# A d-transform with its even half folded a second time, and its copies moved from VectorE to ScalarE

## The chip, the cores and the metric

The kernel runs on one core of one Trainium2 chip. The metric is the device time of one execution in microseconds (us); the median of the runs is given. The profile's engines are PE (TensorE matmuls), PEld (TensorE weight loads), DVE (VectorE), ACT (ScalarE), POOL (GpSimd) and SP (SyncE, which here issues most transfers).

## What is computed

The input x has 2048 rows (time steps) of 1024 columns (d). Two results are made from it and mixed row by row with a gate:

```python
def reference(A_x, A_w_r, A_w_i, B_x, B_Lambda_re, ..., gate_w):
    x = A_x
    g = _sigmoid((x * gate_w).sum(-1, keepdims=True))
    a = irfft2(rfft2(x) * (A_w_r + 1j * A_w_i))        # over rows and columns
    # b: Bu = x @ B_bar^T; h[t] = Lam_bar * h[t-1] + Bu[t]; b = 2 Re(h @ C^T) + x * Dskip
    b = _B_ref(x, B_Lambda_re, ...)
    return g * a + (1 - g) * b
```

Branch a is a spectral filter (a two-dimensional Fourier transform, a product, and the way back). Branch b is a linear recurrence over 2048 steps with 1024 complex states.

## The kernel before

All transforms are matmuls with constant matrices in bf16; sums are in fp32 in PSUM.

**The front of branch a**, about the first 87 us, takes x in 16 row groups of 128 rows, j = 0 to 15. For each group:

- `turn_x(j)`: eight PE transposes (L666) put columns on partitions, into a PSUM tile `pt` (two buffers), and one ACT copy (L667) brings it into `xQ`.
- `fold(j)`: two DVE operations form lo + hi (L674) and lo - hi (L675) of the two halves of d, 128x512 elements each, into a tile `preT` (three buffers). The sum is what the even frequencies need, the difference what the odd ones need.
- `fd(j)`, the d-transform: eight PE matmuls (L346) of 512 columns. For each class (0 even, 1 odd) four blocks of 128 folded columns are multiplied with the constant `G_sb` and summed in one half of the PSUM tile `ps_fd`. A copy (L349) brings it in natural order of frequencies into `X1`; it is on DVE for j = 3, 5, 7 and on ACT for the others.
- `s1(j)`: four PE matmuls (L358), the first step of the transform over rows. A copy (L363) brings it from PSUM into `A1`: on DVE for j below 8, on ACT from 8 on. SP stores A1 to DRAM (L365). The A1 of groups 0 to 7 lie in `CT[0]`, space that x used before; those of 8 to 15 take four places in turn, so that group 12 overwrites group 8. Before that, `keep_A1` (DVE, L369 and L371) saves one column of each into `Acol`.

The PSUM pool `psA` has two buffers, which fd and s1 take in turn: fd(j+1) waits for the copy of fd(j), and s1(j+1) for the copy of s1(j).

**Around it.** The order is written out by hand: `plan` says for each step j of `front()` in which order transposes (T), folds (f), fd(j+1) (F) and s1(j) (S) are issued, and every engine works through its instructions in that order. Among these steps stand the tables of branch b (`make_tab`, four times: DVE L215, L828, L830, L232, L237; ACT L832, L833, L835, L226, L231; casts on POOL, L222 and L228). After step 8, halves of branch b's units are issued in between as well.

**Branch b** is cut into eight chunks of 256 steps. `unit(c, q)` is two times 32 matmuls of 256 columns (L308, `psu`), each followed by an ACT copy (L310). `recur` then queues the DVE work of that chunk (products with the tables, L263 and L266; scans, L278; the way back, L288 and L291). `vector(us)` takes pieces from this queue, by costs written beside them, and so fixes at build time where they stand between the folds. `early(tb)` and the later output tiles read the finished states with PE (`ps_y`, L580); the first such read needs all of chunk 0.

**SP's queue** carries, in order: x and G and T2 (the constant of s1), then the stores of A1 between the transposing loads of B (L207) and C (L565), then the loads of W and of the next constants.

Of the kernel before, what the change touches and what calls it, by code (L numbers as in the profile page):

```python
# [14 lines left out]
BF16 = mybir.dt.bfloat16  # L15
# [22 lines left out]
def _host_consts():  # L38

    d = np.arange(K)[:, None] + 0.5  # L40
    G = np.zeros((2, K, 2, H))
    for cls in range(2):
        k = 2 * np.arange(H)[None, :] + cls
        ang = 2 * np.pi * d * k / D
        G[cls, :, 0] = np.cos(ang)
        G[cls, :, 1] = -np.sin(ang)
    G[0, :, 1, 0] = (-1.0) ** np.arange(K)

    n = np.arange(H)[None, :] + 0.5
    Gi = np.zeros((2, 2, 2, P, H))  # L50
    for cls in range(2):
        for kb in range(2):
            k = 2 * (P * kb + np.arange(P)[:, None]) + cls
            ang = 2 * np.pi * k * n / D
            Gi[cls, kb, 0] = 2.0 * np.cos(ang)
            Gi[cls, kb, 1] = -2.0 * np.sin(ang)
    Gi[0, 0, 0, 0] = 1.0
    Gi[0, 0, 1, 0] = (-1.0) ** np.arange(H)
    Gi /= float(D * S)
    pf = np.arange(P)  # L60
    s1 = (32 * (pf % 64) + 16 * (pf // 64))[:, None, None]
# [36 lines left out]
    return dict(  # L98
        G=b16(G.reshape(2, 4, P, K).transpose(2, 0, 1, 3)),
        Gi=b16(Gi.reshape(8, P, H).transpose(1, 0, 2)),  # L100
        T2=b16(np.concatenate([Ts, Tc, -Ts], axis=2)),
        K3=b16(np.stack([Kc, Ks], axis=1)),
        MT=b16(np.concatenate([-Mim, Mre, Mim], axis=2)),
        KRS=b16(np.concatenate([K2, R2, Sel.reshape(P, 4 * P)], axis=1)),
        JP=b16(np.stack([J, P0], axis=1)),
    )
# [3 lines left out]
def kernel(  # L110
# [17 lines left out]
    nc = tc.nc  # L128
# [4 lines left out]
    cG = nc.inline_tensor(hc["G"], name="c_G").ap()  # L133
# [29 lines left out]
    pre = ictx.enter_context(tc.tile_pool(name="pre", bufs=1, side="right"))  # L163
    gta = ictx.enter_context(tc.tile_pool(name="gta", bufs=2, side="right"))
# [27 lines left out]
    fft["G"] = pre.tile([P, 2, 4, K], BF16, name="G_sb")  # L192
    raw = t3p.tile([P, 6 * D], BF16, name="raw")
    fft["T2"] = raw[:, 0:3 * D].rearrange("p (j m) -> p j m", m=192)

# [141 lines left out]
    def gfnet():  # L337
        T2_sb, G_sb = fft["T2"], fft["G"]
# [2 lines left out]

        def fd(j):
            ps = psA.tile([P, 2, K], FP32, name="ps_fd", tag="ps")
            for cls in range(2):
                for d4 in range(4):
                    nc.tensor.matmul(ps[:, cls, :], lhsT=preTs[j][:, 4 * cls + d4, :], rhs=G_sb[:, cls, d4, :],  # L346
                                     start=(d4 == 0), stop=(d4 == 3))
            X1 = gta.tile([P, 2, K], BF16, name="X1")
            (nc.vector.tensor_copy if j in (3,5,7,) else nc.scalar.copy)(out=X1.rearrange("p r (i c) -> p r i c", c=2), in_=ps.rearrange("p c (r i) -> p r i c", r=2))  # L349
            X1s[j] = X1  # L350

        def s1(j):
            X1 = X1s.pop(j)
            psa = psA.tile([P, 2, K], FP32, name="ps_s1", tag="ps")
            for r in range(2):
                for g in range(2):
                    half = slice(64 * g, 64 * (g + 1))
                    nc.tensor.matmul(psa[:, g, :], lhsT=T2_sb[half, j, 64 - 64 * r:192 - 64 * r], rhs=X1[half, r, :],  # L358
                                     start=(r == 0), stop=(r == 1), tile_position=(64 * g, 0))
# [3 lines left out]
            (nc.vector.tensor_copy if j < 8 else nc.scalar.copy)(out=A1, in_=psa)  # L363
# [294 lines left out]
        yield 3.9  # L658


    preTs = {}

    def turn_x(j):
        pt = psX.tile([P, 8, P], BF16, name="pt")
# [3 lines left out]
                       in_=pt.rearrange("p d (c q g) -> p d c g q", c=NCH, g=2))  # L668

    def fold(j):  # L670
        preTs[j] = gta.tile([P, 8, P], BF16, name="preT", bufs=3)
        lo, hi = (x_gjq[:, :, d:d + 4, :, j, :].rearrange("p c d g q -> p d g c q") for d in (0, 4))
        to = preTs[j].rearrange("p d (g c q) -> p d g c q", g=2, c=NCH)
        nc.vector.tensor_add(out=to[:, 0:4], in0=lo, in1=hi)  # L674
        nc.vector.tensor_sub(out=to[:, 4:8], in0=lo, in1=hi)  # L675
# [308 lines left out]
```

## Time and profile before

| | us |
|---|---|
| median of 3 runs (339.67 to 341.55) | 340.32 |
| the profiled execution | 340.26 |
| its span, first to last instruction | 338.5 |

| engine | busy us | share of the span | instructions |
|---|---|---|---|
| PE | 327.9 | 97% | 2446 |
| PEld | 212.0 | 63% | 2446 |
| DVE | 283.5 | 84% | 385 |
| ACT | 167.3 | 49% | 211 |
| POOL | 32.7 | 10% | 64 |

Busy is the time in which an engine runs an instruction; waiting is not busy. On DVE and ACT an instruction starts shortly before the one ahead of it ends, so what a further one costs is the step from start to start, and not its duration. A line of a timeline gives start, duration, engine, line, operation, output and input, and in brackets how long the engine stood idle before it and who released it. The groups that the change touches:

| line, engine, operation | count | mean or median ns of one |
|---|---|---|
| L346 PE matmul ps_fd, 512 columns | 128 | 379 |
| L308 PE matmul psu, 256 columns | 1024 | 273 |
| L674, L675 DVE preT, 128x512 | 16 + 16 | 417, 418 |
| L349 copy of ps_fd on ACT, 128x1024 | 13 | 1012 |
| L349 copy of ps_fd on DVE | 3 | 1215 |
| L363 copy of ps_s1 on DVE, 128x1024 | 8 | 1218 |
| L363 copy of ps_s1 on ACT | 8 | 1018 |

### The profile page before, as it was taken

How to read it: one execution, taken by the hardware profiler on the slowest of the kernel's cores; microseconds unless marked ns; L12 is line 12 of the kernel's file. 1: busy time of each engine (PE TensorE's matmuls, PEld its weight loads, DVE VectorE, ACT ScalarE, POOL GpSimd, SP SyncE). 2: the span in 40 equal slices, each digit the busy share in tenths (PEclk: the TensorE clock that was granted, in tenths of full speed). 3: DMA queues.
4: the chain of work that ended last, by engine and by line, in shares of the span. 5: the costliest groups of instructions: out<-in, count | busy, mean ns of one | idle time of the engine just before them, and what ended most of it. 6: DMA issues, size and time to landing. Idle time of an engine off the chain costs nothing.

```text
span 338.5 us, 6167 instructions
## 1 busy us (share of the span) xinstructions
PE 327.9 (97%) x2446; PEld 212.0 (63%) x2446; DVE 283.5 (84%) x385; ACT 167.3 (49%) x211; POOL 32.7 (10%) x64
## 2 busy tenths in 40 slices
PE   8989899979999999999999999999999999999995
PEld 3445465656985574847566575869945876565552
DVE  2679948999999999999997999199699939999741
ACT  3697598836241245656557452546632243433510
POOL 1382011140000000000000000000000011121410
PEclk9999999999999999999999999999999999999999
DMA  7999999999890346899999955898114004556892
GB/s 268 404 200 144 244 220 213 129 202 263 261 230 11 95 123 145 254 243 282 259 270 242 218 174 151 225 188 217 62 33 122 35 4 71 102 86 124 131 194 102
DMA packets 83581, 58.71 MB, mean 173 GB/s; under 512 B 54328, under 2 KB 74304, under 8 KB 83424
## 3 DMA queue, kind: packets, MB, share of 16 engines
q1 hardware_dynamic: 80304, 55.64, 66.5%
q0 software_dynamic: 3168, 2.66, 8.3%
q8 instruction: 19, 0.31, 0.4%
q14 instruction: 10, 0.08, 0.1%
q10 hardware_dynamic: 80, 0.01, 0.0%
HBM read 30.49 MB, written 17.83 MB: 143 GB/s over the span
## 4 chain that ended last, share of the span: by engine, by line
PE 81%; DVE 13%; ACT 3%; issue 2%; ACTq 0%; DVEq 0%
PE ps_y L580 29%; PE psu L308 28%; PE ps_h L580 4%; PE ps_id L611 4%; PE ps_fd L346 3%; PE ps_is L519 2%; PE ps_is L494 2%; PE ps_s L470 2%; PE ps_is L495 2%; DVE CT L363 2%; PE ps_y L584 2%; DVE h L278 1%; DVE preT L674 1%; PE psw L684 1%; DVE preT L675 1%
## 5 line engine op out<-in xcount | busy, mean ns | idle before, releaser
L308 PE MATMUL psu<-xQ,BT 128*128 128x256 bf16 x1024 | 116.2, 273 | 0.8 <-ACT ye L598 0.5
L308 PEld LDWEIGHTS <-BT 128*128 128x128 bf16 x1024 | 99.0, 98 | 17.4 <-issue 4.5
L580 PE MATMUL ps_y<-CT,h 128*128 128x512 bf16 x448 | 101.3, 379 | 0.0
L580 PEld LDWEIGHTS <-h 128*128 128x128 bf16 x512 | 49.4, 98 | 55.3
L278 DVE TENSOR_TENSOR_SCAN h<-rz,h 128x1024 bf16<-128x1024 f32 x32 | 71.9, 2278 | 0.2
L310 ACT CAST h<-psu 128x1024 bf16<-128x1024 f32 x32 | 32.3, 1010 | 51.0 <-PE psu L308 51.0
L263 DVE TENSOR_TENSOR xQ<-h,tab 128x4096 bf16<-128x4096 bf16 x12 | 27.4, 2287 | 14.2 <-ACT h L310 14.2
L266 DVE TENSOR_TENSOR h<-h,tab 128x4096 bf16<-128x4096 bf16 (+1 forms) x20 | 37.3, 1864 | 0.8
L626 POOL DMA_DIRECT2D BT<-y_scratch x10 | 11.9, 1194 | 238.8 <-DVE BT L620 227.1
L598 ACT ACTIVATE ye<-ps_y,omg 128x512 f32<-128x512 f32 x20 | 12.7, 684 | 43.4 <-PE ps_y L584 35.7
L346 PE MATMUL ps_fd<-G_sb,preT 128*128 128x512 bf16 x128 | 30.4, 379 | 1.6 <-ACT X L349 1.0
L346 PEld LDWEIGHTS <-preT 128*128 128x128 bf16 x128 | 12.0, 97 | 15.5 <-issue 2.8
L472 ACT CAST X<-ps_s 128x1024 bf16<-128x1024 f32 x16 | 16.2, 1014 | 8.7 <-PE ps_s L470 8.7
L667 ACT COPY xQ<-pt 128x1024 bf16<-128x1024 bf16 x16 | 15.6, 1016 | 2.6 <-PE pt L666 2.5
L521 ACT CAST ZT<-ps_is 128x1024 bf16<-128x1024 f32 x16 | 15.5, 1024 | 2.2 <-PE ps_is L519 2.2
L497 ACT CAST C<-ps_is 128x1024 bf16<-128x1024 f32 x16 | 16.1, 1007 | 0.0
L611 PE MATMUL ps_id<-raw,ZT 128*128 128x256 bf16 x128 | 15.9, 273 | 0.0
L349 ACT CAST X<-ps_fd 128x1024 bf16<-128x1024 f32 x13 | 13.2, 1013 | 5.5 <-PE ps_fd L346 5.4
L580 PE MATMUL ps_h<-CT,h 128*128 128x512 bf16 x64 | 14.5, 379 | 0.0
L611 PEld LDWEIGHTS <-ZT 128*128 128x128 bf16 x128 | 12.4, 98 | 2.2
L674 DVE TENSOR_TENSOR preT<-xQ 128x512 bf16<-128x512 bf16 x16 | 7.4, 460 | 5.8 <-ACT xQ L667 5.8
L494 PE MATMUL ps_is<-X,raw 128*128 128x512 bf16 x32 | 12.1, 379 | 0.0
(189 smaller groups left out, 350.0 us busy)
## 6 DMA issues: line engine op xcount, KB each, us to landing
y_scratch<-ye SPq DMA_DIRECT2D x20, 256.0 KB, 2.7
CT<-in_A_x_dram SPq DMA_DIRECT2D x8, 512.0 KB, 5.6
Bb<-turn_scratch SPq DMA_DIRECT2D x16, 256.0 KB, 3.8
turn_scratch<-C SPq DMA_DIRECT2D x16, 256.0 KB, 4.5
raw<-turn_scratch SPq DMA_DIRECT2D x16, 256.0 KB, 4.7
Wb<-in_A_w_r_dram SPq DMA_DIRECT2D x32, 127.8 KB, 4.0
Wb<-in_A_w_i_dram SPq DMA_DIRECT2D x32, 127.8 KB, 3.8
out_dram<-BT SPq DMA_DIRECT2D x14, 256.0 KB, 2.6
```

What stands on the lines that cost most here:

```text
L263: nc.vector.tensor_mul(out=tmps["s"], in0=u[:, ::-1], in1=bc(i))
L266: nc.vector.tensor_mul(out=u, in0=u, in1=bc(i))
L278: nc.vector.tensor_tensor_scan(out=seg, data0=rz[:, js.start + j:js.start + j + 4].rearrange("p j t -> p (j t)"), data1=seg, initial=0.0, ...
L308: nc.tensor.matmul(psu[:, j, :], lhsT=BT[4 * q + j][:, ri, d8, :], rhs=xQ[:, c, d8, :], start=(d8 == 0), stop=(d8 == 7))
L310: nc.scalar.copy(out=hs[c][:, ri, 4 * q:4 * q + 4].rearrange("p b (q j) -> p b q j", j=32), in_=psu.rearrange("p b (j q) -> p b q j", j=32))
L346: nc.tensor.matmul(ps[:, cls, :], lhsT=preTs[j][:, 4 * cls + d4, :], rhs=G_sb[:, cls, d4, :], start=(d4 == 0), stop=(d4 == 3))
L472: nc.scalar.copy(out=X2, in_=ps2)
L494: nc.tensor.matmul(psc[:, h, :], lhsT=MT_sb[:, b, 64:192], rhs=UV[0][:, h, :], start=True, stop=False)
L497: nc.scalar.copy(out=C1.rearrange("p h (c i) -> p h c i", c=2), in_=psc.rearrange("p h (i c) -> p h c i", c=2))
L580: nc.tensor.matmul(psy, lhsT=hs[c][:, ri, jb, P * tq:P * (tq + 1)], rhs=CT[ri][:, jb, 512 * dh:512 * (dh + 1)], start=(i == 0), stop=False)
L611: nc.tensor.matmul(pse[:, slot, :], lhsT=ZT_t[:, i, tb, :], rhs=fft["Gi"][:, i, :], start=(kb == 0), stop=(kb == 1))
L667: nc.scalar.copy(out=x_gjq[:, :, :, :, j, :].rearrange("p c d g q -> p d c g q"), in_=pt.rearrange("p d (c q g) -> p d c g q", c=NCH, g=2))
```

## The change

The even frequencies are split once more. From the sum s = lo + hi (four blocks of 128 columns) a second fold makes s_lo + s_hi, for the frequencies 4m, and s_lo - s_hi, for 4m + 2. Each of the two needs only two blocks and gives 256 outputs. The even half of fd thus becomes four matmuls of 256 columns in place of four of 512; the odd half stays, and now comes first. The constant `G_sb` is laid out anew, and its second transfer is half as large (256 KB). The copy into `X1` reads PSUM in a new order (two by two, from both classes and both even parts).

The second fold is done for two groups at once: for groups 0 and 1 two operations of 128x256 each, and from then on two operations of 128x2x256 after every odd group. fd of an even group therefore waits for the fold of the next group. `preT` becomes a tile for two groups (two buffers), and the sums have a tile of their own (one buffer).

All X1 copies are on ACT (before, 3, 5 and 7 were on DVE), and the A1 copies of groups 1, 3, 5, 7 too (before, all below 8 were on DVE). `plan` is as it was.

```diff
-                nc.tensor.matmul(ps[:, cls, :], lhsT=preTs[j][:, 4 * cls + d4, :], rhs=G_sb[:, cls, d4, :],
-                                 start=(d4 == 0), stop=(d4 == 3))
+            for d4 in range(4):
+                nc.tensor.matmul(ps[:, 1, :], lhsT=preTs[j][:, 4 + d4, :], rhs=Go[:, d4, :], start=(d4 == 0), stop=(d4 == 3))
+            for e in range(2):
+                for d2 in range(2):
+                    nc.tensor.matmul(ps[:, 0, H * e:H * (e + 1)], lhsT=preTs[j][:, 2 * e + d2, :], rhs=Ge[:, e, d2, :],
+                                     start=(d2 == 0), stop=(d2 == 1))
...
-            (nc.vector.tensor_copy if j in (3,5,7,) else nc.scalar.copy)(out=X1.rearrange("p r (i c) -> p r i c", c=2), in_=ps.rearrange("p c (r i) -> p r i c", r=2))
+            (nc.vector.tensor_copy if j in () else nc.scalar.copy)(
+                out=X1.rearrange("p r (m e c) -> p r m e c", e=2, c=2),
+                in_=ps.rearrange("p c (e r m) -> p r m e c", e=2, r=2))
...
-            (nc.vector.tensor_copy if j < 8 else nc.scalar.copy)(out=A1, in_=psa)
+            (nc.vector.tensor_copy if j in (0, 2, 4, 6) else nc.scalar.copy)(out=A1, in_=psa)
...
     def fold(j):
-        preTs[j] = gta.tile([P, 8, P], BF16, name="preT", bufs=3)
+        if j % 2 == 0:
+            pairs["t"] = gta.tile([P, 2, 8, P], BF16, name="preT", bufs=2)
+            pairs["s"] = gta.tile([P, 2, 4, P], BF16, name="sums", bufs=1)
+        preTs[j] = pairs["t"][:, j % 2]
         lo, hi = (x_gjq[:, :, d:d + 4, :, j, :].rearrange("p c d g q -> p d g c q") for d in (0, 4))
-        to = preTs[j].rearrange("p d (g c q) -> p d g c q", g=2, c=NCH)
-        nc.vector.tensor_add(out=to[:, 0:4], in0=lo, in1=hi)
-        nc.vector.tensor_sub(out=to[:, 4:8], in0=lo, in1=hi)
+        apart = lambda t: t.rearrange("p d (g c q) -> p d g c q", g=2, c=NCH)
+        nc.vector.tensor_sub(out=apart(preTs[j])[:, 4:8], in0=lo, in1=hi)
+        nc.vector.tensor_add(out=apart(pairs["s"][:, j % 2]), in0=lo, in1=hi)
+        rs = slice(j % 2, j % 2 + 1) if j < 2 else slice(0, 2)
+        if j < 2 or j % 2:
+            s_lo, s_hi = pairs["s"][:, rs, 0:2], pairs["s"][:, rs, 2:4]
+            nc.vector.tensor_add(out=pairs["t"][:, rs, 0:2], in0=s_lo, in1=s_hi)
+            nc.vector.tensor_sub(out=pairs["t"][:, rs, 2:4], in0=s_lo, in1=s_hi)
...
-    for cls in range(2):
-        nc.sync.dma_start(out=fft["G"][:, cls], in_=cG[:, cls])
+    for part in (slice(0, 4 * K), slice(4 * K, 4 * K + 4 * H)):
+        nc.sync.dma_start(out=fft["G"][:, part], in_=cG[:, part])
```

More of the change, by code (lines that the diff above doesn't have):

```diff
@@ L47, in _host_consts @@
     G[0, :, 1, 0] = (-1.0) ** np.arange(K)
+    Ge = np.stack([G[0, :H, :, e::2] for e in range(2)])
+    Go = np.stack([G[1, :, :, e::2] for e in range(2)], axis=1)
     n = np.arange(H)[None, :] + 0.5
@@ L98, in _host_consts @@
     return dict(
-        G=b16(G.reshape(2, 4, P, K).transpose(2, 0, 1, 3)),
+        G=b16(np.concatenate([Go.reshape(4, P, 4 * K // 4).transpose(1, 0, 2).reshape(P, 4 * K),
+                              Ge.reshape(2, 2, P, H).transpose(2, 0, 1, 3).reshape(P, 4 * H)], axis=1)),
         Gi=b16(Gi.reshape(8, P, H).transpose(1, 0, 2)),
@@ L191 @@
     fft = {}
-    fft["G"] = pre.tile([P, 2, 4, K], BF16, name="G_sb")
+    fft["G"] = pre.tile([P, 4 * K + 4 * H], BF16, name="G_sb")
     raw = t3p.tile([P, 6 * D], BF16, name="raw")
@@ L343, in fd @@
             ps = psA.tile([P, 2, K], FP32, name="ps_fd", tag="ps")
-            for cls in range(2):
-                for d4 in range(4):
-                    nc.tensor.matmul(ps[:, cls, :], lhsT=preTs[j][:, 4 * cls + d4, :], rhs=G_sb[:, cls, d4, :],
-                                     start=(d4 == 0), stop=(d4 == 3))
+            Go = G_sb[:, 0:4 * K].rearrange("p (d n) -> p d n", d=4)
+            Ge = G_sb[:, 4 * K:4 * K + 4 * H].rearrange("p (e d n) -> p e d n", e=2, d=2)
+            for d4 in range(4):
[4 more added lines that the diff above has]
+                                     start=(d2 == 0), stop=(d2 == 1))
             X1 = gta.tile([P, 2, K], BF16, name="X1")
-            (nc.vector.tensor_copy if j in (3,5,7,) else nc.scalar.copy)(out=X1.rearrange("p r (i c) -> p r i c", c=2), in_=ps.rearrange("p c (r i) -> p r i c", r=2))
+            (nc.vector.tensor_copy if j in () else nc.scalar.copy)(
+                out=X1.rearrange("p r (m e c) -> p r m e c", e=2, c=2),
+                in_=ps.rearrange("p c (e r m) -> p r m e c", e=2, r=2))
             X1s[j] = X1
@@ L658, in own_tile @@
         yield 3.9
-    preTs = {}
+    preTs, pairs = {}, {}
     def turn_x(j):
@@ L687 @@
     load_x(0)
-    for cls in range(2):
-        nc.sync.dma_start(out=fft["G"][:, cls], in_=cG[:, cls])
+    for part in (slice(0, 4 * K), slice(4 * K, 4 * K + 4 * H)):
+        nc.sync.dma_start(out=fft["G"][:, part], in_=cG[:, part])
     load_T2(0, 2)
```

## The prediction

> **What bounds the kernel now.** I read the engines' busy times first, then the chain that ended last, then busy times by stage, then the timelines of the stages in which PE, DVE or ACT waits. Head of the page and chain view:
>
> ```profile
> PE 327.9 (97%) x2446; PEld 212.0 (63%) x2446; DVE 283.5 (84%) x385; ACT 167.3 (49%) x211; POOL 32.7 (10%) x64
> ...
> PE 81%; DVE 13%; ACT 3%; issue 2%; ACTq 0%; DVEq 0%
> ```
>
> PE is 97% busy, so PE work taken out ought to shorten the end. But 13% of the chain is DVE, and the chain in order of time puts nearly all of that before 72 us. Busy times by stage (columns: length; PE, PEld, DVE, ACT, POOL busy; clock; DMA):
>
> ```profile
> 16.20:37.00 20.80, 19.33 (x160) 10.40 (x158) 18.93 (x50) 18.31 (x26) 9.51 (x17) 1.00 1.20 196
> 37.00:43.80 6.80, 5.84 (x44) 3.93 (x44) 5.07 (x13) 3.33 (x6) 0.61 (x1) 1.00 1.00 216
> 43.80:51.70 7.90, 7.90 (x56) 4.75 (x56) 4.05 (x11) 7.61 (x13) 1.22 (x2) 1.00 1.07 206
> 51.70:72.80 21.10, 19.41 (x164) 12.49 (x161) 20.79 (x32) 14.29 (x22) 5.23 (x10) 1.00 1.12 185
> 72.80:101.50 28.70, 28.69 (x262) 23.30 (x261) 27.25 (x41) 13.09 (x15) 0.11 (x1) 1.00 1.00 244
> ```
>
> From 16 to 37 us DVE (91%) and ACT (88%) are as full as PE; from 51.7 to 72.8 DVE is full (20.79 of 21.10) and PE is not. What ends that stage stands in the timelines of DVE, ACT and PE:
>
> ```profile
> 51.67 1.23 DVE L263 TENSOR_TENSOR su<-h,tab 128x2048 bf16<-128x2048 bf16 x1 [2.18 <-ACT h L310]
> ...
> 58.10 0.39 DVE L674 TENSOR_TENSOR preT<-xQ 128x512 bf16<-128x512 bf16 x1
> ...
> 70.42 0.83 DVE L674 TENSOR_TENSOR preT<-xQ 128x512 bf16<-128x512 bf16 x1
> 71.17 0.41 DVE L675 TENSOR_TENSOR preT<-xQ 128x512 bf16<-128x512 bf16 x1
> 71.50 0.17 DVE L371 COPY Acol<-A 128x8 bf16<-128x8 bf16 x1
> ```
> ```profile
> 41.38 0.63 ACT L832 ACTIVATE rot_kk<-ang 128x512 f32<-128x512 f32 x1 [3.48 <-DVE ang L830]
> ...
> 71.75 1.01 ACT L363 CAST A<-ps_s 128x1024 bf16<-128x1024 f32 x1 [4.43 <-DVE Acol L371]
> ```
> ```profile
> 69.22 1.89 PE L346 MATMUL ps_fd<-G_sb,preT 128*128 128x512 bf16 x8
> 72.81 0.61 PE L358 MATMUL ps_s<-X,raw 64*128 64x512 bf16 x4 [1.70 <-ACT A L363]
> ```
>
> So the path is: ACT's copy of the first unit's second half (L310, 50.58) starts DVE at 51.67; DVE runs without a gap to Acol at 71.50, behind the folds of groups 13, 14 and 15; Acol releases ACT's A1(12), that releases s1(13) at 72.81. From there PE has no gap to 260 us. **The end therefore moves as s1(13) moves, less what PE saves after it.**
>
> **The change part by part.**
>
> *PE, fd.* Eight 512-column matmuls step 1.73 us (the chain's 17.08 to 18.82), 0.216 each. A 256-column one steps 0.110 (psu: 32 from 46.18 to 49.69). New: 4 x 0.216 + 4 x 0.110 = 1.30, a saving of 0.43 per group, 6.9 over 16. Only fd(15), the one behind 72.81, is free of the path above: 0.43.
>
> *DVE, folds.* A 512-element fold steps 0.335 (16.54, 16.87). Each later pair gains two of the same element count (0.67) and one wait for DVE's own result; that wait costs 0.12, as dependent small operations step 0.20 (24.12, 24.32) where free ones step 0.08 (24.41, 24.48). So **0.79 per pair**. Bounds: 0.67 if the wait is hidden; 1.2 if both run like the fold at 70.42 (0.83 busy, 0.41 over the others) because POOL casts beside them. The row without POOL is nearest in shape: 0.79. Groups 0 and 1 pay some 0.5 each for four half-size operations; the stage in front of fd(1) covers it.
>
> *Copies.* X1 copies 3, 5, 7 (L349) and A1 copies 1, 3, 5, 7 (L363) leave DVE, 7 x 1.13 = 7.9 us, and go to ACT at its step of 0.90, 6.3 us. The new X1 copy reads PSUM in another order. Unknown; below: the present one (also strided) takes 1.012, as a plain cast does (L472, 1.014). Above: the slowest ACT copy, zsb (L714), takes 1.10 for 512 elements, hence some 2.2 for 1024. I take 1.01, the row nearest in size and type.
>
> [...]
>
> *The start.* G's second transfer halves (512 to 256 KB), so the 0.29 that fd(0) lost (2.02 against 1.73) should go; fd(0) and fd(1) save 0.43 each. Transpose 2 then runs at 10.44 instead of 11.49. Going on row by row, fold pair (2,3) ends at 14.6 and fd(2), now waiting for it, at 15.25; X1(2) starts on ACT at 15.3 instead of 16.29 and its next work at 16.17, **1.0 ahead**.
>
> *16 to 38 us.* From 16.17 ACT holds, up to the end of the first table's scaled copies (36.90 before): eleven transpose copies and X1(3) to X1(7), 16 x 0.90 = 14.4; A1(3), A1(5), 1.8; table load and small functions 0.23 + 1.28 + 0.12 + 0.22; the table chain 0.53 + 0.52 + 0.62 + 1.60. Sum 21.3, so it ends at 37.5, **0.6 later than before**, if ACT never waits. It does not: each X1 copy finds its fd done (closest: fd(6), behind fold pair (6,7) at 27.0, is done at 28.65; ACT takes it at 28.8). PE now waits for ACT (fd(8) for X1(7), 34.5; fd(9) for X1(8), 38.56 instead of 37.96), so its saving here is lost.
>
> *38 to 51 us.* DVE continues from the scaled copies: tab, fold 10, tab, ang. Before, A1(7) stood in between (1.13). So ang ends at 41.35 + 0.57 - 1.13 = 40.78, 0.57 sooner, and ACT's rot_kk (41.38, waiting for it) with all that follows: X1(9), A1(8), t, tab, ang, rot_kk, sn_f. L310's second half would start at 50.0 instead of 50.58. PE is not later: its second unit ends at 49.4 (38.56 + 1.39 + 0.54 + 3.5 + 1.39 + 0.54 + 3.5). DVE starts at 51.1, **0.58 sooner**.
>
> *51 to 73 us.* DVE has the same work plus the second folds of (12,13) and (14,15), both ahead of Acol: 2 x 0.79 = 1.58. Acol: 71.50 - 0.58 + 1.58 = 72.50; s1(13): 72.81 + 1.0 = 73.8. Behind Acol wait ACT's A1(12), L310 and X1(14). New waits of PE lie beside this one: fd(12) needs the pair of fold(13) (about 59.1; PE is there near 57.6), fd(14) that of fold(15) (about 72.4). They cost nothing more, since s1(13) is later than both; without Acol, fd(14) would still hold PE to 73.
>
> *73 us to the end.* PE: +1.0 - 0.43 = **+0.57**. Cover on other queues: DVE reaches the first ps_y read at 100.9 (99.92 + 1.0), PE at 102.06 (101.49 + 0.57), where 1.6 of slack was; DVE then waits for g_bf (0.59 idle before), which takes up the other 0.43. SP's A1(9) store stands behind two fewer C transposes than before (issue 74.04, landing some 3.3 later), so A1(13), which waited 3.0 for it, loses that wait; it was not what held PE.
>
> **Sum.** The profiled execution took 340.26 (span 338.5 and 1.76 around it), 0.06 below the median of 340.32. 340.26 + 0.57 = **340.8 us**. The front's sums may be off by about 1 us either way, the pair price by -0.2 to +0.8 over two pairs: own range 339.3 to 342.4.
>
> **Rivals.**
>
> *PE's saving reaches the end.* For it: PE's 97% and 81%. If pairs and copies all hide, fd(10) to fd(15) give 6 x 0.43 = 2.6 and the 1.70 stall goes: 336.0; with all 16 groups and no stall, 340.26 - 6.9 - 1.7 = 331.7. Against it: 20.79 of 21.10 on DVE, and PE already waiting there. A milder form: DVE's start comes 2 us or more sooner than I sum, giving 338.5 or less.
>
> *ACT becomes the bound of the front.* One mechanism: the reordered X1 read. At zsb's rate each copy costs 1.1 more; X1(3) to X1(7) lie in ACT's gapless stretch and X1(8), X1(9) behind it, 7 x 1.1 = 7.7: 348.5. It decides from about 0.15 us per copy on (1.1 over seven copies, which with 0.57 makes 1.7). For it: zsb's row. Against it: L349 and L472. A weak form (ACT waits for late folds that I have as done, 1.5 to 3 us) gives 342.3 to 344.
>
> *The clock falls in the longer gaps.* Before, the longest PE gap past 7 us was 1.70 and the clock 1.00 throughout. Now PE would wait about 2.5 at fd(14) and 0.7 at s1(13). By rows: from nothing up to a doubled time of the psu behind it (3.5 more): 344.3.
>
> [...] No row here shows a lowered clock.
>
> **How the numbers follow.** Runs of this kernel tell about 0.5% from no change, 1.7 us. Forecast (338.6 to 342.0): 0.56. PE's saving reaches the end, mild or full: 0.16. ACT bounds the front, weak or strong: 0.20. Clock: 0.08. The last two lie above 342.0: slower 0.28, faster 0.16, same 0.56. The range leaves out the full PE gain and the strong ACT case (together under 0.2): 337.5 to 344.5.
>
> **What would show it.** Right: X1 copies on ACT near 1.01; ACT without gaps from 16 to 37.5; the second folds near 0.42 busy; L310's second copy near 50.0; Acol near 72.5 and PE's stall before s1(13) and in fd(14) together above 3 us; no gap from there to 259 us. Wrong: s1(13) before 71.5 (faster), X1 copies above 1.15 or a clock below 1.00 (slower), or PE gaps behind 73 us.

## The result, and the profile after

Four runs of the changed kernel took 343.76 to 344.63 us, median 344.19; the kernel before took 340.26 (median) beside it. Ratio 1.011, 95% interval 1.0078 to 1.0143: the change made the kernel slower by about 1.1%. The time lies inside the range of the prediction, but not inside the forecast's own (339.3 to 342.4). The profiled execution is 344.63 with a span of 342.8, 4.3 more than before.

The page's head, the slices of the granted clock and the shares of the chain:

```profile
PE 324.7 (95%) x2416; PEld 213.0 (62%) x2446; DVE 282.7 (82%) x396; ACT 173.7 (51%) x218; POOL 32.9 (10%) x64
...
PEclk9999699998999999999999999999999999999999
...
PE 86%; ACT 7%; DVE 3%; issue 3%; ACTq 0%; DVEq 0%
```

PE is busy 3.2 us less (the fd saving of 6.9, less what lower speed gave back; 30 of its 2446 matmul records are missing after), and the span is longer all the same. New is the second line: two slices show a clock below full, one near 35 to 43 us and one near 77. Before had 1.00 throughout. Of the chain, DVE's 13% became 3%: what ends last in the front is now PE at half speed and PE's waits for ACT. Busy times by stage, the same stretches as before, then stretches of 3.41 us that end or begin where the clock changes (columns: length; PE, PEld, DVE, ACT, POOL busy; clock; DMA):

```profile
16.20:37.00 20.80, 16.12 (x139) 9.68 (x142) 13.79 (x46) 20.77 (x29) 9.68 (x17) 0.97 1.15 194
37.00:43.80 6.80, 5.72 (x29) 2.44 (x25) 5.74 (x15) 5.64 (x10) 0.69 (x1) 0.60 1.13 223
51.70:72.80 21.10, 19.19 (x166) 12.49 (x166) 19.72 (x28) 14.25 (x21) 4.56 (x7) 1.00 1.17 157
72.80:101.50 28.70, 26.28 (x227) 20.80 (x228) 27.94 (x41) 11.66 (x12) 0.33 (x4) 0.94 0.99 246
...
32.19:35.60 3.41, 1.26 (x7) 0.48 (x5) 1.23 (x1) 3.41 (x6) 0.61 (x1) 1.00 0.84 209
35.60:39.01 3.41, 2.22 (x10) 0.78 (x9) 2.26 (x6) 3.41 (x8) 0.61 (x1) 0.50 0.94 185
69.73:73.15 3.42, 1.78 (x12) 1.01 (x11) 3.35 (x4) 0.00 (x0) 0.00 (x0) 1.00 1.34 117
73.15:76.56 3.41, 1.34 (x9) 0.51 (x10) 3.38 (x9) 1.68 (x2) 0.33 (x4) 1.00 1.22 287
76.00:80.00 4.00, 4.00 (x21) 2.60 (x21) 3.86 (x5) 2.64 (x3) 0.11 (x1) 0.57 1.00 233
```

ACT is full from 16 to 37 us (20.77 of 20.80), as forecast. PE is busy 1.26 of 3.41 us just before the clock falls at 35.6, and 1.34 of 3.41 just before it falls at 76.6. After 1.78 of 3.42 it did not fall. The first fall lasts 6.8 us, two such stretches, the second 3.4. PE's timeline (start, duration, ..., in brackets the idle time before and who ended it) shows where the gaps are and what half speed costs:

```profile
34.84 0.81 PE L350 MATMUL ps_fd<-G_sb,preT 128*128 128x512 bf16 x3 [2.15 <-ACT X L356]
35.75 1.06 PE L353 MATMUL ps_fd<-G_sb,preT 128*128 128x256 bf16 x4
36.74 1.04 PE L367 MATMUL ps_s<-X,raw 64*128 64x512 bf16 x4
38.86 1.87 PE L350 MATMUL ps_fd<-G_sb,preT 128*128 128x512 bf16 x4 [1.08 <-ACT X L356]
...
42.48 3.67 PE L311 MATMUL psu<-xQ,BT 128*128 128x256 bf16 x32
...
74.43 0.72 PE L353 MATMUL ps_fd<-G_sb,preT 128*128 128x256 bf16 x4 [2.87 <-DVE preT L691]
75.94 0.61 PE L367 MATMUL ps_s<-X,raw 64*128 64x512 bf16 x4 [0.79 <-ACT A L372]
76.49 5.33 PE L311 MATMUL psu<-xQ,BT 128*128 128x256 bf16 x32
```

fd(9)'s four 512-column matmuls take 1.87 where fd(10)'s take 1.03; s1(8) 1.04 for 0.61; the psu behind s1(13) 5.33 for 3.67. So the first unit starts at 42.48 (40.32 before), and its late end passes through ACT to DVE:

```profile
40.88 0.63 ACT L849 ACTIVATE rot_kk<-ang 128x512 f32<-128x512 f32 x1 [1.16 <-DVE ang L847]
...
51.62 1.01 ACT L313 CAST h<-psu 128x1024 bf16<-128x1024 f32 x1 [1.16 <-PE psu L311]
...
74.88 1.01 ACT L372 CAST A<-ps_s 128x1024 bf16<-128x1024 f32 x1 [5.71 <-issue]
```
```profile
52.73 1.23 DVE L266 TENSOR_TENSOR su<-h,tab 128x2048 bf16<-128x2048 bf16 x1 [3.74 <-ACT h L313]
...
68.97 1.68 DVE L266 TENSOR_TENSOR su<-h,tab 128x2048 bf16<-128x2048 bf16 x1
...
73.16 0.42 DVE L686 TENSOR_TENSOR preT<-xQ 128x512 bf16<-128x512 bf16 x1
73.50 0.41 DVE L687 TENSOR_TENSOR sums<-xQ 128x512 bf16<-128x512 bf16 x1
73.95 0.42 DVE L691 TENSOR_TENSOR preT<-sums 128x512 bf16<-128x512 bf16 x1
74.29 0.41 DVE L692 TENSOR_TENSOR preT<-sums 128x512 bf16<-128x512 bf16 x1
74.63 0.18 DVE L380 COPY Acol<-A 128x8 bf16<-128x8 bf16 x1
```

DVE starts at 52.73 (51.67 before) and reaches Acol 21.90 us later (19.83 before): 1.58 for the two second folds and 0.5 more, net, from operations that are longer while POOL works beside them (L266 1.68 for 1.23). Acol is at 74.63 for 71.50, s1(13) at 75.94 for 72.81. The 4.3 us are 3.1 up to s1(13), plus 1.66 in the slow psu, less the 0.43 of fd(15).

### The profile page after: what moved, and what is told of

It reads as the page before. It is cut to its first block, busy times and chain, and to the rows that moved or that the text cites. A ratio compares the mean times of both kernels' runs of the same rounds, so it can differ in the third digit from the quotient of the medians.

```text
span 342.8 us, 6163 instructions
## 1 busy us (share of the span) xinstructions
PE 324.7 (95%) x2416; PEld 213.0 (62%) x2446; DVE 282.7 (82%) x396; ACT 173.7 (51%) x218; POOL 32.9 (10%) x64
## 4 chain that ended last, share of the span: by engine, by line
PE 86%; ACT 7%; DVE 3%; issue 3%; ACTq 0%; DVEq 0%
PE psu L311 32%; PE ps_y L589 28%; PE ps_h L589 4%; PE ps_id L620 4%; ACT xQ L676 3%; PE ps_is L503 2%; PE ps_fd L350 2%; PE ps_is L528 2%; PE ps_is L504 2%; PE ps_y L593 2%; ACT X L356 2%; PE ps_s L367 2%; PE ps_s L479 2%; PE ps_fd L353 1%; PE psw L701 1%
## 5 line engine op out<-in xcount | busy, mean ns | idle before, releaser
L311 PE MATMUL psu<-xQ,BT 128*128 128x256 bf16 x1024 | 117.9, 275 | 0.8 <-ACT ye L607 0.5
L311 PEld LDWEIGHTS <-BT 128*128 128x128 bf16 x1024 | 100.0, 99 | 18.6 <-issue 4.5
L589 PE MATMUL ps_y<-CT,h 128*128 128x512 bf16 x436 | 99.5, 379 | 0.6
L313 ACT CAST h<-psu 128x1024 bf16<-128x1024 f32 x32 | 32.4, 1012 | 56.0 <-PE psu L311 55.9
L266 DVE TENSOR_TENSOR xQ<-h,tab 128x4096 bf16<-128x4096 bf16 x12 | 27.4, 2287 | 14.2 <-ACT h L313 14.2
L350 PE MATMUL ps_fd<-G_sb,preT 128*128 128x512 bf16 x57 | 16.6, 396 | 4.5 <-ACT X L356 3.8
L356 ACT CAST X<-ps_fd 128x1024 bf16<-128x1024 f32 x16 | 16.7, 1041 | 3.7 <-PE ps_fd L353 3.6
L676 ACT COPY xQ<-pt 128x1024 bf16<-128x1024 bf16 x16 | 16.4, 1055 | 1.5 <-PE pt L675 1.4
L353 PE MATMUL ps_fd<-G_sb,preT 128*128 128x256 bf16 x64 | 10.9, 292 | 3.8 <-DVE preT L691 3.6
L266 DVE TENSOR_TENSOR su<-h,tab 128x2048 bf16<-128x2048 bf16 x8 | 10.2, 1278 | 3.8 <-ACT h L313 3.7
L350 PEld LDWEIGHTS <-preT 128*128 128x128 bf16 x64 | 5.9, 99 | 11.1 <-issue 6.7
```

Source lines behind the costliest of these rows:

```text
L266: nc.vector.tensor_mul(out=tmps["s"], in0=u[:, ::-1], in1=bc(i))
L311: nc.tensor.matmul(psu[:, j, :], lhsT=BT[4 * q + j][:, ri, d8, :], rhs=xQ[:, c, d8, :], start=(d8 == 0), stop=(d8 == 7))
L313: nc.scalar.copy(out=hs[c][:, ri, 4 * q:4 * q + 4].rearrange("p b (q j) -> p b q j", j=32), in_=psu.rearrange("p b (j q) -> p b q j", j=32))
L350: nc.tensor.matmul(ps[:, 1, :], lhsT=preTs[j][:, 4 + d4, :], rhs=Go[:, d4, :], start=(d4 == 0), stop=(d4 == 3))
L356: (nc.vector.tensor_copy if j in () else nc.scalar.copy)(out=X1.rearrange("p r (m e c) -> p r m e c", e=2, c=2), in_=ps.rearrange("p c (e ...
L589: nc.tensor.matmul(psy, lhsT=hs[c][:, ri, jb, P * tq:P * (tq + 1)], rhs=CT[ri][:, jb, 512 * dh:512 * (dh + 1)], start=(i == 0), stop=False)
```

## The experiments

Theory A: the clock, which in the changed kernel fell behind stretches of 3.41 us with 1.26 and 1.34 us of PE work and not behind one with 1.78, is most of the loss; the rest is the second folds ahead of Acol. Theory B, the rival: the lateness of ACT and DVE is the loss itself, and the clock only a symptom of it. The kernel before ran beside each group and took 340.57, 340.73, 340.44 and 340.57 us (for runs 1 to 4, 5 to 8, 9 to 11, and 12). One half-speed window of 3.41 us (clock 0.50, as from 35.60 to 39.01 above) lowers the mean clock of a run by 0.005 (0.5 x 3.41 / 340), so a run's mean clock tells how many it had: the profiled run of the changed kernel has 0.985, three.

| run | edit | median us | ratio to before, 95% |
|---|---|---|---|
| e1 | changed + matmuls in three gaps | 341.09 | 1.0005 (0.9980 to 1.0029) |
| e2 | second fold alone | 344.48 | 1.0108 (1.0092 to 1.0125) |
| e3 | copies alone | 342.36 | 1.0052 (1.0037 to 1.0067) |
| e4 | changed, fold 15 and Acol early | 343.63 | 1.0089 (1.0074 to 1.0104) |
| e5 | changed, X1(7) on DVE | 342.25 | 1.0047 (1.0021 to 1.0073) |
| e6 | e1 with few matmuls | 343.03 | 1.0057 (1.0030 to 1.0083) |
| e7 | e1, last gap alone | 342.10 | 1.0037 (1.0015 to 1.0058) |
| e8 | e5 + unit begun earlier | 339.46 | 0.9968 (0.9947 to 0.9988) |
| e9 | before + unit begun earlier | 341.87 | 1.0026 (1.0007 to 1.0044) |
| e10 | changed, no second fold for groups 12 to 15 | 341.34 | 1.0008 (0.9988 to 1.0029) |
| e11 | e8 + e10 | 340.17 | 0.9984 (0.9957 to 1.0010) |
| e12 | e10 + matmuls in the front gaps | 339.96 | 0.9976 (0.9959 to 0.9993) |

### e1: work for PE in the gaps

Matmuls that nothing reads: nine of 512 columns ahead of fd(8) and of fd(9), twelve between the halves of fd(14).

```diff
+FILL1 = {8: 9, 9: 9}
+FILL2 = {14: 12}
...
+            if j in FILL1:
+                fill = (psF if j < 9 else pools["u"]).tile([P, 2, K], FP32, name="fill", tag="psu")
+                for i in range(FILL1[j]):
+                    nc.tensor.matmul(fill[:, i % 2, :], lhsT=ident, rhs=Go[:, 0, :], start=True, stop=True)
             for d4 in range(4):
                 nc.tensor.matmul(ps[:, 1, :], lhsT=preTs[j][:, 4 + d4, :], rhs=Go[:, d4, :], start=(d4 == 0), stop=(d4 == 3))
+            for i in range(FILL2.get(j, 0)):
+                nc.tensor.matmul(ps[:, 0, :], lhsT=ident, rhs=Go[:, 0, :], start=True, stop=True)
```

> The changed kernel with matmuls added whose results nobody reads: 9 of 512 columns ahead of fd(8) and of fd(9), 12 between the halves of fd(14), where PE waited 2.2, 1.1 and 2.9 us. Theory A (most of the loss is a lowered clock after those waits): clock 1.000, no stretch at half speed, ACT's second L310 copy near 50.0 instead of 51.6, s1(13) near 74.0 instead of 75.9, time near 340.9 us (344.2 less 1.6 and 1.7). Theory B (ACT and DVE are late by themselves and the clock only shows it): the clock recovers, but the time stays above 343.

Measured 341.09, 3.1 below the changed kernel, with PE doing more work. PE's timeline in front, DVE's start, and s1(13):

```profile
32.45 2.12 PE L354 MATMUL fill<-G_sb,ident 128*128 128x512 bf16 x8
34.67 1.02 PE L356 MATMUL ps_fd<-G_sb,preT 128*128 128x512 bf16 x4
...
36.60 2.12 PE L354 MATMUL fill<-G_sb,ident 128*128 128x512 bf16 x9
38.69 1.02 PE L356 MATMUL ps_fd<-G_sb,preT 128*128 128x512 bf16 x4
```
```profile
51.00 1.23 DVE L268 TENSOR_TENSOR su<-h,tab 128x2048 bf16<-128x2048 bf16 x1 [2.19 <-ACT h L315]
```
```profile
73.59 0.61 PE L375 MATMUL ps_s<-X,raw 64*128 64x512 bf16 x4 [0.74 <-ACT A L380]
```

fd(8) still starts at 34.67 and fd(9) at 38.69, when ACT has copied; but fd(9) takes 1.02 and not 1.87, DVE starts at 51.00 (the prediction had 51.1), Acol is at 72.27 (72.50) and s1(13) at 73.59 (73.8). So theory B is wrong for the greater part: ACT and DVE wait as they did, and 3.1 us are gone. With the clock full the change costs 0.52 (341.09 against 340.57); the forecast's sum was 0.57. The interval of the ratio reaches from -0.7 to +1.0 us, so the two agree within the noise and no closer.

### e6 and e7: how little is enough, and one fall at a time

e6 has two matmuls in each of the three gaps, e7 the twelve in fd(14) alone.

The edit of e6 against e1 (e7 has `{}` and `{14: 12}`):

```diff
-FILL1 = {8: 9, 9: 9}
-FILL2 = {14: 12}
+FILL1 = {8: 2, 9: 2}
+FILL2 = {14: 2}
```

> The changed kernel with only two unread 512-column matmuls in each of the gaps at fd(8), fd(9) and fd(14) (0.43 us each time, where the first filler kernel had nine, nine and twelve). By the busy times of the changed kernel this lifts the window ahead of the first fall from 1.25 to about 1.68 us of 3.40 (49%), and the one ahead of the second from 1.28 to 1.71 (50%). Theory A with a threshold below one half (38% fell, 51% in the kernel with the copies alone did not): clock 1.00 throughout, 340.8 to 341.6. If it is the length of one gap that counts (2.15 us at fd(8), 2.87 at fd(14), here 1.7 and 2.4), or the threshold lies above one half, the clock falls as before and the time is 343.5 to 344.5.

> The changed kernel with the twelve unread matmuls in the gap of fd(14) alone; the front as changed. Theory A: the first fall (35.5 to 42.4) stays, the second goes, and psu behind s1(13) takes 3.67 again in place of 5.33: 1.7 below the changed kernel, 342.3 to 342.8; first ps_y read near 104.2. If the two falls are not separate costs (the end is set by DVE, which no filler makes faster), the time stays within 0.5 of the changed kernel, 343.7 to 344.5.

e6's ten runs spread, and sort by the mean clock: 340.68 and 341.00 at 0.999 to 1.000 (no half-speed window); 341.88, 342.86, 343.03 and 343.03 at 0.993 to 0.995 (one); 343.60 to 344.16 at 0.990 (two). The edit is the same in all ten; that they differ by where the windows lie against the gaps is inferred, since only one of them has a trace. A half-speed window costs 1 to 2 us here. The profiled run of e6 had one, from 72.47; its two emptiest windows were:

```profile
69.06:72.47 3.41, 1.22 (x6) 0.37 (x4) 3.34 (x7) 0.00 (x0) 1.16 (x3) 1.00 1.26 189
31.52:34.93 3.41, 1.79 (x17) 0.75 (x15) 1.42 (x2) 3.41 (x6) 0.61 (x1) 1.00 0.85 185
```

At fd(14) the two matmuls came ahead of the wait and the window still held 1.22 us of PE work: the clock fell. In front 1.79 of 3.41 was enough. Neither of the two expected outcomes came for the whole; both did, run by run.

e7's median came just below what theory A expects, 342.10 for 342.3 to 342.8. In the profiled run the psu behind s1(13) takes 3.67 again, a fall in front is still there (40.5 to 43.9), and the first ps_y read is at 103.82 (104.2 expected, 105.86 in the changed kernel). The median mixes two kinds of runs, which was not expected: four of the ten have a mean clock of 1.000, so no fall at all (341.49 to 341.90); five have one or two half-speed windows (342.30 to 343.32); and one with a single window took 340.22, which nothing here explains. Without the late fall the one in front thus costs about 1 us, and the falls are separate costs. The profiled run also shows that the place of the windows matters: PE waits 2.15 us at fd(8), as in the changed kernel, but across the border of two windows, counted back in steps of 3.41 us from the fall at 40.47. The first holds 1.81 of 3.41 us of work and brings no fall; the clock falls one window later, behind 1.39 of 3.41 ahead of fd(9).

### e2 and e3: one part of the change alone

e2 is the changed kernel with the copies as before:

```diff
-            (nc.vector.tensor_copy if j in () else nc.scalar.copy)(
+            (nc.vector.tensor_copy if j in (3, 5, 7) else nc.scalar.copy)(
...
-            (nc.vector.tensor_copy if j in (0, 2, 4, 6) else nc.scalar.copy)(out=A1, in_=psa)
+            (nc.vector.tensor_copy if j < 8 else nc.scalar.copy)(out=A1, in_=psa)
```

e3 is the kernel before with the copies as in the change:

```diff
-            (nc.vector.tensor_copy if j in (3,5,7,) else nc.scalar.copy)(out=X1.rearrange("p r (i c) -> p r i c", c=2), in_=ps.rearrange("p c (r i) -> p r i c", r=2))
+            (nc.vector.tensor_copy if j in () else nc.scalar.copy)(out=X1.rearrange("p r (i c) -> p r i c", c=2), in_=ps.rearrange("p c (r i) -> p r i c", r=2))
...
-            (nc.vector.tensor_copy if j < 8 else nc.scalar.copy)(out=A1, in_=psa)
+            (nc.vector.tensor_copy if j in (0, 2, 4, 6) else nc.scalar.copy)(out=A1, in_=psa)
```

> The second fold alone: copies on DVE and ACT as before. Theory A: DVE, full in the front already, gets four pairs more there (4 x 0.79 = 3.2 us, some of it hidden), so ang and L310 come about 2 us later than before, Acol another 1.6: 343 to 346 us, with PE waits that may lower the clock. Theory B (the moved copies are what costs): near 339, below before.

> The kernel before with only the copies moved to ACT as in the change; no second fold. Theory A: ACT ends its scaled copies about 1.6 us later than before, DVE saves 1.13 on the way, nothing is added ahead of Acol, PE's waits stay short because fd still takes 1.73: clock 1.000, 340 to 341.5 us. Theory B: 343 or more.

e2 took 344.48. Two of its waits of PE (us in total, times, longest):

```profile
PE ps_fd L353 <- DVE preT L691: 5.0, 4, 2.6
PE ps_s L367 <- DVE CT L372: 3.8, 5, 1.6
```

With the copies on DVE as before, the second folds make DVE the late one already in front (3.8 us of waits for A1 copies), DVE's su starts at 53.68 and s1(13) is at 76.53; one fall of the clock, at 77.3, behind a window with 1.48 of 3.41 busy. So the second fold alone costs as much as the whole change.

e3 took 342.36, above the 340 to 341.5 that was expected, with the clock full in the profiled run. PE waited for ACT's X1 copies:

```profile
36.26 1.89 PE L346 MATMUL ps_fd<-G_sb,preT 128*128 128x512 bf16 x7 [1.59 <-ACT X L349]
...
40.28 1.02 PE L346 MATMUL ps_fd<-G_sb,preT 128*128 128x512 bf16 x4 [1.59 <-ACT X L349]
```

That put fd(9) 2.3 later than before (40.28 for 37.96), DVE's su at 53.32 and s1(13) at 75.13. The expectation counted DVE's chain only. The parts (+3.9 and +1.8 against the kernels beside them) do not add up to the whole (+3.9). A reading that fits e2's and e3's waits, but that no run tests apart, is that the copies relieve the DVE that the folds load, and that the shorter fd relieves the front that the copies load.

### e4: fold 15 and the columns early

Fold 15 is issued right behind fold 14, and Acol's columns 8 to 11 behind s1(11), so that neither stands in front of s1(13).

```diff
-            if j in (8, 12):
-                keep_A1(j - 4)
+            if j == 8:
+                keep_A1(4)
...
-    plan = {0: "FSTfTf", 1: "TSFfT", 2: "TFfTS", 3: "TFfTS", 4: "TFfTS", 5: "TFfTS", 6: "TFfTS", 7: "TFfTS"}
+    plan = {0: "FSTfTf", 1: "TSFfT", 2: "TFfTS", 3: "TFfTS", 4: "TFfTS", 5: "TFfTS", 6: "TFfTS", 7: "TFfTS", 11: "ffFS"}
...
+        if j == 11:
+            fft["keep"](8)
```

> The changed kernel with fold 15 issued right behind fold 14 and Acol of groups 8 to 11 saved right after s1(11), ahead of the queued work of branch b. Theory A: the 2.9 us wait in fd(14) and the wait ahead of s1(13) go, and with them the second stretch at half speed; the first stays. PE then reaches the first ps_y read before DVE has chunk 0 done (103.1), so that DVE sets it: 105.86 becomes about 103.1, time near 341.4 us. Theory B: no more than 1 us is won, as PE meets DVE's lateness elsewhere.

Measured 343.63, 2.2 above what theory A expected. s1(13) starts at 71.93 without a wait and the first ps_y read at 100.18 (105.86 in the changed kernel), but then:

```profile
106.95 0.56 PE L439 MATMUL zps<-Bcol,K_sb 32*128 32x16 bf16 x16 [2.92 <-DVE Bcol L432]
```
```profile
103.73:107.14 3.41, 0.49 (x13) 0.41 (x12) 3.31 (x6) 0.00 (x0) 0.00 (x0) 1.00 0.02 3
```

PE meets the same late DVE at Bcol, waits 2.92 there, and the clock falls behind that window (0.49 of 3.41 busy). The front's fall is there as in the changed kernel (35.5 to 42.3). Here theory B's form holds: DVE is full from 52 us on, and an earlier s1(13) only moves the wait.

### e10 and e12: fewer second folds, and both cures at once

e10 makes the second fold for groups 0 to 11 only. Groups 12 to 15 write four sums straight into `preT`, and the even half of fd takes eight 256-column matmuls, with a negated copy of two blocks of the constant (128 KB more). e12 adds the front fillers of e1.

```diff
+NRAD4 = 12
...
+        if j >= NRAD4:
+            nc.vector.tensor_add(out=apart(preTs[j])[:, 0:4], in0=lo, in1=hi)
+            return
...
+            else:
+                Gn = G_sb[:, 4 * K + 4 * H:4 * K + 6 * H].rearrange("p (d n) -> p d n", d=2)
+                for e in range(2):
+                    for d4 in range(4):
+                        nc.tensor.matmul(ps[:, 0, H * e:H * (e + 1)], lhsT=preTs[j][:, d4, :],
+                                         rhs=Gn[:, d4 - 2, :] if e and d4 > 1 else Ge[:, e, d4 % 2, :], start=(d4 == 0), stop=(d4 == 3))
```

> The changed kernel with the second fold for groups 0 to 11 only: groups 12 to 15 form their four sums at once and take eight 256-column matmuls in the even half (a negated copy of two blocks, 128 KB more of the constant), 0.43 us more of PE per group. If the two second folds ahead of Acol cost the 1.58 us of the prediction and make fd(14) wait: Acol near 73.0 in place of 74.63, fd(14) without its wait for the pair, the wait before s1(13) below 2.5 us, so no second fall of the clock, psu 3.67 again: 344.2 - 1.6 - 1.7 + 0.4 = 341.3 (340.8 to 342.3; where the front's fall is missing too, 339.8). If DVE's full queue simply fills with the next work (the folds are not what Acol waits for), Acol moves by under 0.5 and the time is 343 or more.

> The changed kernel with both of its losses taken away by separate edits: the second fold for groups 0 to 11 only (Acol 2.3 us sooner, no second fall of the clock, measured alone), and nine unread 512-column matmuls each in the gaps at fd(8) and fd(9) (no first fall, as in the run with all fillers). If the two losses are separate and add up: su near 51.0 as in that run, Acol 19.8 behind it, near 70.9 (69.9 to 72 with POOL's collisions), clock 1.00 throughout, Bcol near 103.5, and the time is 339.6 (339.0 to 340.2), some 1.7 below the run with the mixed folds alone and 1.5 below the run with the fillers alone. If DVE's full queue from 51 to 104 gives the gain back, by a wait of PE at Bcol of 1 us or more and a fall of the clock behind it, the time is 340.5 to 341.5.

e10 took 341.34 (341.3 expected). DVE, then PE:

```profile
71.23 0.82 DVE L696 TENSOR_TENSOR preT<-xQ 128x512 bf16<-128x512 bf16 x1
71.98 0.41 DVE L698 TENSOR_TENSOR preT<-xQ 128x512 bf16<-128x512 bf16 x1
72.32 0.17 DVE L389 COPY Acol<-A 128x8 bf16<-128x8 bf16 x1
```
```profile
73.63 0.61 PE L376 MATMUL ps_s<-X,raw 64*128 64x512 bf16 x4 [1.42 <-ACT A L381]
74.17 3.67 PE L313 MATMUL psu<-xQ,BT 128*128 128x256 bf16 x32
```

From su (52.50) to Acol it takes 19.82, as before (19.83), where the changed kernel took 21.90. fd(14) does not wait, only 1.42 is left before s1(13), and the clock does not fall there. The front's fall (35.3 to 42.1) is as in the changed kernel. e10's runs spread too: nine with two half-speed windows took 341.06 to 341.77, three with one took 339.08, 339.35 and 341.87. e12 took 339.96 (339.6 expected, 339.0 to 340.2): su 50.87, Acol 70.57, Bcol 103.59 (103.5 expected), clock 1.00, no wait at Bcol. So in the medians the front's fall and the folds ahead of Acol, with the fall behind them, are two losses that add up: 344.19, less 2.85 (e10), less 1.38 more (e12). The two runs of e10 near 339 are as short as e12's shortest (339.34) with one window at half speed; what sets them apart is open.

### e5, e8, e9 and e11: real work in the front gap

e5 puts X1(7) back on DVE. e8 adds to it the first half of the first unit right behind s1(7), so that PE works through its wait for X1(8); eight halves stay in the front. e9 moves the same half in the kernel before (X1(7) is on DVE there anyway), e11 in e10 with X1(7) on DVE.

```diff
-            (nc.vector.tensor_copy if j in () else nc.scalar.copy)(
+            (nc.vector.tensor_copy if j in (7,) else nc.scalar.copy)(
...
-        if j >= 8:
+        if 8 <= j < 15:
             halves(ssm, 1)
...
             pools["u"] = ctx.enter_context(tc.tile_pool(name="psU", bufs=2, space=PSUM, reuse_waits="tile"))
+            halves(ssm, 1)
```

> The changed kernel with one copy back on DVE: X1(7), the one that PE waited for in fd(8). Theory A (the clock falls after a window of about 3.4 us in which PE is busy less than some 40 to 50%, and the two falls cost 1.6 and 1.7 us): DVE can take X1(7) at 31.9, behind the second folds, and end it at 33.1; fd(8) then starts at 33.1 in place of 34.84, but ACT still brings X1(8) only at 36.8, so that PE idles some 2.7 us before fd(9). The wait is moved, not gone: the window ahead of fd(9) holds about 1 us of PE work, the clock still falls, between 36 and 43 us, and the time is 343 to 344. Theory B (the extra copies on ACT are the cost themselves, the clock is a symptom of the wait at fd(8)): with one copy less and fd(8) free, the copies' cost shrinks by a quarter or more and the clock stays full in front: 341.5 to 342.5.

> The changed kernel with real work in the front gaps: X1(7) on DVE, and the first half of the first unit issued right behind s1(7), so that PE works through its wait for X1(8); the halves issued in the front stay eight in all (the one behind step 15 goes). No work is added. Theory A: PE runs from fd(8) at 33.1 without a long gap, clock 1.00, fd(9) near 38.6, the first unit complete by 44 and not 51; DVE no longer waits for its h and starts su near 48 in place of 52.7, Acol near 70, s1(13) near 71; then PE meets DVE at Bcol, near 102.4 (105.3 in the kernel before): 337 to 339. If B's weights are not there in time, or DVE's work in the front rather than the late unit holds its start, su starts at 50 or later and the time is 340 or more.

> The kernel before, with nothing of the change, but the first half of the first unit issued right behind s1(7) as in the run with real work in the gaps (X1(7) is on DVE in it anyway; eight halves in the front, as ever). It tells whether that run's gain belongs to the earlier unit or to the second fold. If the earlier unit alone brings it: DVE's su starts right behind the table's ang, near 49.4 in place of 51.67, Acol near 69.3 (up to 1.5 later if POOL's descriptors and casts meet the folds), Bcol near 102.2 in place of 104.5, and the time is 337.5 to 338.5, below the changed kernel with the same edit (339.46), since no second fold stands on DVE's path. If the second fold has its share (PE's shorter fd), this kernel stays at or above 339.5.

> Both edits in the changed kernel: second fold for groups 0 to 11 only, X1(7) on DVE, and the first half of the first unit issued behind s1(7). If the front's gap, the fall of the clock and the two folds ahead of Acol were all that the change lost: su near 48.9, Acol near 70.1, no wait in fd(14) and no fall, and Bcol near 102.4 (104.0 without the first edit), so that the end is 1.6 below the run with real work in the gaps: 337.9 (337 to 338.6), and level within 0.7 with the kernel before under the same edit. If the second fold for the first twelve groups is worth something at the end, it is below that kernel by 1 us or more; if their second folds still cost, above it by 1 or more.

e5: median 342.25, in theory B's span, but its runs fall into two groups, 341.29 to 342.30 at a clock of 0.994 to 0.995 and 343.64 to 344.13 at 0.985 to 0.989. In the profiled run the front's fall is gone, since the one long wait became four short ones (0.40 at fd(8), 0.52 in it for the second folds, 0.74 at s1(7), 1.24 at fd(9); the emptiest window has 1.75 of 3.41 busy), and the fall at fd(14) stayed (73.2). Theory A had expected one wait of 2.7 at fd(9), which was wrong. As a test between A and B it decides nothing.

e8: 339.46 beside 340.73. PE, then DVE:

```profile
36.02 0.61 PE L367 MATMUL ps_s<-X,raw 64*128 64x512 bf16 x4 [0.74 <-DVE CT L372]
36.56 3.67 PE L311 MATMUL psu<-xQ,BT 128*128 128x256 bf16 x32
40.06 1.03 PE L350 MATMUL ps_fd<-G_sb,preT 128*128 128x512 bf16 x4
```
```profile
48.89 1.22 DVE L266 TENSOR_TENSOR su<-h,tab 128x2048 bf16<-128x2048 bf16 x1
```

DVE starts 3.8 earlier than in the changed kernel and waits for no h; but it reaches Acol only at 71.64 (70 expected); operations beside POOL's descriptors and casts are longer there (folds of 1.22 and 0.71 for 0.41). PE waits 1.11 at Bcol. The clock was expected at 1.00, and it did not stay there: in the profiled run it falls at fd(14) (72.9 to 76.3, behind 1.51 of 3.41), and nine of the ten runs have one half-speed window. They took 339.17 to 341.08, the one run without took 339.37, so here a window cost nothing that shows.

e9: 341.87, not the 337.5 to 338.5 that the earlier unit alone was to bring. Its other answer came, that the time stays at or above 339.5. But e8 differs from e9 in the second fold and in the copies that are on ACT, so the share is that of both together, and part of the difference is a fall of the clock in e9 (below). In e9 PE reaches s1(13) at 74.07 with 0.36 of waiting, so PE itself holds this stage, and the longer fd delays ACT (X1 copies wait 0.71 for fd twice, at 54.20 and 62.01) and through it DVE (1.94 idle for the table's `t` at 66.02). Then:

```profile
105.34 0.54 PE L430 MATMUL zps<-Bcol,K_sb 32*128 32x16 bf16 x16 [2.24 <-DVE Bcol L423]
```

The clock fell behind this window (1.17 of 3.41 busy). Three of the twelve runs kept 1.000 and took 340.02 to 340.56, the others 341.71 to 342.29.

e11: 340.17 (337 to 338.6 expected; the interval of its ratio holds 1). s1(13) is at 72.88, 1.2 before e9's; DVE idles 1.83 for `t` at 64.95, as in e9, so Bcol is at 103.89 and not 102.4. PE waits 2.23 there, the same as in e9, and in the profiled run the clock stayed at 1.00. The runs at 0.998 to 1.000 took 338.17 to 339.13, the others 339.99 to 342.44.

e8 and e12 are faster than both kernels: 0.3% and 0.2% below the kernel before, with intervals that exclude 1, though under the 0.5% named in the prediction and small for the best two of twelve.

## Why the prediction was right and wrong

**PE, fd: right.** fd(10) steps 1.40 (45.98 to 47.38) where it stepped 1.82 (43.82 to 45.64): 0.42 saved, 0.43 forecast.

**Second folds: right.** 1.58 for two pairs; e10 took them away and won back 2.08 between su and Acol, of which 0.5 is operations that were longer while POOL worked beside them, as the range allowed for.

**Copies: right.** X1 copies take 1.04 in the mean, 1.01 to 1.02 mostly. Between 22 and 39 us they take up to 1.15, but so do the transpose copies between them (1.16), and the step from one to the next stays 0.90. At that step the strided read costs nothing that shows.

**16 to 38 us: the times right, the price wrong.** ACT is gapless to 37.66 (37.5 forecast), fd(8) waits until 34.84 (34.5) and fd(9) until 38.86 (38.56). The prediction wrote of these waits only "so its saving here is lost". The first holds PE at 1.26 busy of 3.41 us, and the clock falls behind it.

**38 to 73 us: right but for the clock.** rot_kk at 40.88 (40.78). L310's second copy (L313 after) was forecast at 50.0 and came at 51.62, Acol at 74.63 for 72.50. With the clock full (e1) DVE starts at 51.00, Acol is at 72.27, s1(13) at 73.59: all within 0.25 of the forecast.

**The sum: right at full clock, as far as it can be told.** +0.57 forecast, +0.52 in e1, with an interval of -0.7 to +1.0; e7's four runs at full clock lie 0.8 to 1.2 above the kernel beside them.

**The step that failed is the rival "The clock falls in the longer gaps".** It was given 0.08, and it is what happened, as the sign that the prediction named for it (a clock below 1.00) shows. Two things were wrong in it. It looked only at the waits at fd(14) and s1(13), whose lengths it had nearly right (2.5 and 0.7 forecast, 2.87 and 0.79 measured): the fall in front, at fd(8), came first, and it made DVE 1.7 later (52.73 against 51.00 in e1). And it judged by the length of one idle stretch, where the busy share of a window sorts the profiled runs. The clock fell behind windows of 3.41 us with 0.49 and 1.26 (e4), 1.17 (e9), 1.22 (e6), 1.26 and 1.34 (changed), 1.26 (e10), 1.35 (e5), 1.39 (e7), 1.48 (e2) and 1.51 us (e8) of PE work, that is 14 to 44%. It did not fall behind 1.75 (e5), 1.78 (changed), 1.79 (e6), 1.81 (e7) and 1.88 (e2), 51 to 55%. The length of a gap does not sort them: the windows at fd(14) that brought a fall in the changed kernel, e2, e5 and e8 hold two pieces of idle time, neither longer than 1.27 us, while one piece of 1.6 alone (changed at 69.7, e6, e7) brought none. The bound, somewhere between 44 and 51%, is not pinned closer. The price of 344.3 came out right by chance: one doubled psu of 3.5 was meant, which no run shows; the runs show a clock of 0.50 for 3.4 or 6.8 us, the psu behind s1(13) at 5.33 for 3.67, and two falls that cost some 1.7 each. So it is the width that the range gave to its rivals, and not the forecast's own path, that holds 344.19.

The two falls of the changed kernel begin 40.96 us apart (35.63 and 76.59, worked out from the clock in slices of 0.3 us: 0.72 from 35.5, 0.98 from 76.3), twelve times 3.413. In e6, e7, e9 and e11 the mean clock shows falls in some runs of a kernel and not in others (e9: 1.000 in three runs, 0.993 to 0.995 in nine). That the windows follow each other whatever PE does is inferred from these figures, and no run tests it.

**After 73 us: the cover was named wrongly.** The text said that DVE reaches the first ps_y read with 1.6 of slack. The operation at 99.92 belongs to chunk 1. Chunk 0 was complete with the L291 at 84.07, so that read has some 16 us of slack. The place where PE next meets DVE is Bcol (DVE 104.51, PE 105.27 before). This did no harm to the sum, but it is the wait that took back the gains of e4, e9 and e11.

Open: that POOL's work is what lengthens DVE's operations is only read from their coinciding; no run took POOL's work away.

## What to carry to other kernels

Where a change shortens PE's work but not what PE waits for, it makes gaps; add up PE's busy time in each 3.4 us around them, and where it comes near one half (here the clock fell behind 0.49 to 1.51 of 3.41 us, and not behind 1.75 or more), price the next one or two windows at half speed, for PE and for all that waits on PE (1 to 2 us in e6; in e8 nothing that shows). Before taking an operation out of PE, look for work to put in its place: the same fold that cost 1.1% was 0.3% below the kernel before once a unit's half stood in the gap and one copy was back on DVE. And extra work on an engine that was full (two second folds on DVE ahead of Acol, 1.58 us; 2.08 won back in e10) was paid in full, so make it only for the groups where that engine has room.

## What was not expected of the hardware

- Matmuls that nobody reads made the kernel 3.1 us faster (e1), since they kept the clock at 1.00.
- The clock fell while PE was up to 44% busy in the window (1.51 of 3.41), and came back after one window or two (3.4 or 6.8 us): a half-speed window with 2.22 to 2.53 us busy (changed, e4, e10) was followed by a second one, one with 2.93 (e6) or more was not.
- The kernel before shows the fall too in a few runs: of the 90 beside the experiments, eight had a mean clock of 0.990 to 0.995 and took 342.13 to 344.60, the others 339.90 to 342.25. Its profiled run has no fall, but a stretch of 3.41 us around its longest wait (69.6 to 73.0) holds 1.71 us of PE work, 50%.
- Small DVE operations beside POOL's descriptors and casts took several times as long: `ck` (L287) 0.61 and `carry` (L288) 0.87 at 67.5 to 69 us of the changed kernel, where their medians are 0.20 and 0.18. `carry` starts at 68.18 and ends at 69.05; POOL's descriptors run from 67.20 to 68.41, its cast from 68.40 to 69.02. `carry` and the cast end within 0.03 us of each other, but `carry` starts 0.22 ahead, and no run tested whether one held the other up.
